# Written order on four more engines in the attention loop of a fused retention and mixture-of-experts kernel

## The chip, the cores and the metric

The kernel runs on one core of a Trainium2 chip. The metric is the device time of one execution in microseconds. Before the change three runs took 645.19, 640.9 and 643.24 us, median 643.24. A profile, taken of one more execution, lists every instruction of the five engines: TensorE (PE, with its weight loads as PEld), VectorE (DVE), ScalarE (ACT), GpSimd (POOL) and the load queue SyncE (SP), and the transfers of the DMA engines.

## The reference

Retention (a causal attention with a decay by distance in place of softmax) over 8 batches, 8 heads, 576 positions and 64 dimensions, then a mixture of experts over the 4608 resulting tokens of width 512, with 8 experts and one expert for each token:

```python
scores = scale * np.matmul(q, k.transpose(0, 1, 3, 2))
Dmat = np.where(rel >= 0, gamma[:, None, None] ** rel[None, :, :], 0.0)
x = np.matmul(scores * Dmat[None], v)          # then (B*S, H*D)
xn = x / (norm(x) + 1e-6); en = emb / (norm(emb) + 1e-6)
logits = xn @ en.T / tau
expert_idx = np.argmax(logits, axis=1)
gate_w = softmax(logits)[expert_idx]
out[mask_e] = gate_w * (relu(x[mask_e] @ w1[e]) @ w2[e])
```

All arithmetic is in float32.

## The kernel before, in words

**The attention loop** runs over the batches b = 0 to 7, and inside a batch over four pairs of heads. A pair of q and k, transposed, is one tile `qkt` of 576 KB (`load_qk`, L447); eight such tiles exist, so that batch b+1 loads into those of batch b-1. K and V in row form come as one transfer each (`load_k` L455, 1024 KB; `load_v` L460, 1152 KB), two buffers each.

For each pair, TensorE multiplies k and q in 128-wide chunks (`emit_A`, L590) into PSUM, and VectorE multiplies by the decay within a chunk (L599), which gives the masked scores in a `raw` tile. GpSimd scales q by its decay (`scale_q`, L579) in place, once A has read it. `emit_U` (L617; `emit_U0`, L639, in batch 0) forms k times v for each chunk, where k has been scaled by GpSimd (`scale_k`, L560, four steps; in batch 0 `turn_k`, L568 and L570, makes it from `qkt`). ScalarE copies the first chunk's result to `Tst` (L627, L647) and VectorE adds up the others (L629, L649). `emit_O` (L673) multiplies the masked scores by v, `emit_S` (L689) adds the state times scaled q, for two pairs at a time, and ScalarE copies x out (L699 to L702). The last 64 positions go apart: `emit_At` (L711, reads scaled q of all four pairs), its mask `pt` on VectorE (L713), `emit_Ot` (L728), copies L738.

**The router** works behind, in slots of the next two batches (`route_slots`): transposes of x tiles (`route_tile`, L754), a ScalarE copy to `y` (L758), a store to memory (L760, 256 KB each), sums of squares (L768), logits with the normalised expert matrix E (`route_logits`, L781, copies L784), a turn and sum (`route_turn`, L794, L797), the `head` (`route_head`, L174 to L182: seven small VectorE steps that find the best expert), then ranks (`route_rank`, L233 to L260), one-hots (`route_onehot`, L268 to L283), and a table (`route_table`, L296, L305, L307). E is made in batch 0 by `norm_E` (sum of squares, L534 to L538) and `build_E` (a GpSimd power L541, then VectorE L542 to L545). GpSimd's `build_g` (L520) makes the table `gsb` that `scale_q` uses.

In batches 3 to 6 one block of expert 0's first weight is loaded each (`w0_load`, L437), and split into two parts a batch later as written (`w0_split`: ScalarE cast L442, VectorE L443).

**The expert part** follows: for each expert, gathers, two chains of matmuls (L391, L951) and a scatter.

What sets the order: TensorE's instructions in the attention loop run in the order in which the code is written (`tc.manual_schedule` with TensorE alone). For the other engines and the load queue a planner picks among the instructions by its own estimate of what is ready; on the chip each engine then works through its list in order. All loads are issued from the SP queue, which is in order too: a transfer that must wait for a free buffer holds those behind it.

Of the kernel before, what the change touches and what calls it, by code (L numbers as in the profile page):

```python
# [18 lines left out]
P = 128  # L19
B, H, S, D = 8, 8, 576, 64  # L20
# [60 lines left out]
def retention_moe(ctx: ExitStack, tc: tile.TileContext, qk, kv, w1, w2, head, cst, out):  # L81
# [344 lines left out]
    with ExitStack() as att:  # L426
# [12 lines left out]
        def w0_split(c):  # L439
            hi, lo = (wslot[0][:, s, c * 1024 : (c + 1) * 1024] for s in range(2))  # L440
            raw = w0.pop(c)
            nc.scalar.copy(hi, raw)  # L442
            nc.vector.tensor_tensor(out=lo, in0=raw, in1=hi.bitcast(F32), op=ALU.subtract)  # L443

        def load_qk(b, p):
            t = qkp.tile([P, 2, S], F32, name="qkt")
            nc.sync.dma_start(out=t, in_=qk[b, p])  # L447
            qkt[b, p] = t

        kt, vt_ = {}, {}  # L450
# [13 lines left out]
        emb = cs[:, _FIRST : _FIRST + NP * NE].rearrange("p (r e) -> p r e", r=NP)  # L464
        taub = cs[:, _FIRST + NP * NE :]

        def load_decay(o, w):
            nc.sync.dma_start(out=cd[:, o : o + w], in_=cst[:, o : o + w])

        load_qk(0, 0)  # L470
        nc.sync.dma_start(out=cs, in_=head)
        load_decay(0, 2 * P)
        load_qk(0, 1)
        o = _C["g1"][0] - _FIRST
        load_decay(o, _CST.shape[1] - o)
        load_decay(2 * P, 2 * P)
        vt_[0] = a2.tile([P, KW + NP * D], F32, name="vt")
        v0 = vt_[0][:, :KW].rearrange("p (c n) -> p c n", c=NCH)
        v1 = kv[0, :, KW : 2 * KW].rearrange("p (c n) -> p c n", c=NCH)
        nc.sync.dma_start(out=v0[:, :, : DM // 2], in_=v1[:, :, : DM // 2])  # L480
        load_qk(0, 2)
        load_qk(0, 3)
        load_decay(4 * P, 4 * P + _C["decayt"][1])
        nc.sync.dma_start(out=v0[:, :, DM // 2 :], in_=v1[:, :, DM // 2 :])
        nc.sync.dma_start(out=vt_[0][:, KW:], in_=kv[0, :, 2 * KW :])
# [54 lines left out]
        def build_E():  # L540
            nc.gpsimd.tensor_tensor(out=en, in0=en, in1=half[:, :NE], op=ALU.pow)  # L541
            nc.vector.tensor_scalar(out=en, in0=en, scalar1=1e-6, scalar2=taub, op0=ALU.add, op1=ALU.mult)  # L542
            nc.vector.reciprocal(en, en)
            for p in range(NP):
                nc.vector.tensor_tensor(out=E32[:, p, :NE], in0=emb[:, p, :], in1=en, op=ALU.mult)  # L545
# [61 lines left out]
        def emit_U(b):  # L607
            k, v, T = kview(b), vview(b), Tst
            for c2 in range(NCH // 2):
                ps = psm.tile([P, 512], F32, name="m")  # L610
                u = ps.rearrange("p (c r d) -> p c r d", c=2, r=NP)
                for ci in range(2):
                    c = 2 * c2 + ci
                    for p in range(NP):
                        for h in range(2):
                            hd = 2 * p + h
                            nc.tensor.matmul(  # L617
                                u[h * D : (h + 1) * D, ci, p, :],
                                k[:, c, hd * D : (hd + 1) * D],
                                v[:, c, hd, :],  # L620
                                start=True,
                                stop=True,
                            )
                for ci in range(2):
                    c = 2 * c2 + ci
                    if c == 0:
                        nc.scalar.copy(T[:, 0], u[:, 0])  # L627
                    else:
                        nc.vector.tensor_tensor(out=T[:, c], in0=u[:, ci], in1=T[:, c - 1], op=ALU.add)  # L629
# [175 lines left out]
        def route_slots(b):  # L805

            G = group_tiles(b)[1]
            tiles = [lambda g=g: route_tile(b, g) for g in range(G)]
            rank, onehot = (lambda: route_rank(b)), (lambda: route_onehot(b))
            table, head = (lambda: route_table(b)), (lambda: route_head(b))  # L810
            logits, turn = (lambda: route_logits(b)), (lambda: route_turn(b))
            sq = route_squares
            if b == B - 2:
                gathers = [lambda i=i: gather(0, i, group_tiles(B - 1)[0] * P) for i in range(3)]
                return {
                    (b, 3): [logits] + tiles[:2] + [sq],
                    (b + 1, 0): [turn] + tiles[2:3] + [head, sq],
                    (b + 1, 1): [rank] + tiles[3:] + [sq],
                    (b + 1, 2): [onehot],
                    (b + 1, 4): [table, lambda: slots_to_tokens(0, 3)] + gathers + [route_bump],  # L820
                }
            return {
                (b + 1, 0): [logits] + tiles[:2] + [sq],
                (b + 1, 2): tiles[2:3] + [turn, head, sq],
                (b + 1, 3): tiles[3:] + [sq],
                (b + 2, 0): [rank, onehot],
                (b + 2, 2): [table],
            }

# [4 lines left out]
        def slot(b, k):  # L834
            for task in slots.pop((b, k), ()):
                task()

        ordered = tc.manual_schedule(engines={mybir.EngineType.PE})
        ordered.__enter__()
        for b in range(B):  # L840
            if b + 1 < B:
                load_qk(b + 1, 0)
                load_qk(b + 1, 1)
                load_v(b + 1)
                load_k(b + 1)
            if b == 0:
                build_g(0)
                build_g(1)
                emit_A(0, 0)
                turn_k(0)  # L850
                scale_q(0, 0)
                norm_E()
                emit_A(0, 1)
                turn_k(1)
                scale_q(0, 1)
                build_g(2)
                build_g(3)
                emit_O(0, 0)
                emit_U0(0)
                for p in (2, 3):  # L860
                    emit_A(0, p)
                    turn_k(p)
                    scale_q(0, p)
                build_E()
            else:
                for p in (0, 1):
                    emit_A(b, p)
                    scale_q(b, p)
                slot(b, 0)
                emit_U(b)  # L870
                emit_O(b, 0)
            if b >= 4:
                w0_split(b - 4)
            emit_S(b, 0)
            if b + 1 < B:
                load_qk(b + 1, 2)
                load_qk(b + 1, 3)
                scale_k(b + 1)
            if 3 <= b < 7:
                w0_load(b - 3)  # L880
            slot(b, 1)
            if b > 0:
                for p in (2, 3):
                    emit_A(b, p)
                    scale_q(b, p)
            slot(b, 2)
            emit_O(b, 1)
            if b == 0:
                emit_U0(1)
            slot(b, 4)  # L890
            emit_At(b)
            emit_S(b, 1)
            emit_Ot(b)
            slot(b, 3)
# [318 lines left out]
```

## Time and profile before

| What | Value |
|---|---|
| Runs, median (lowest to highest) | 643.24 us (640.9 to 645.19) |
| Profiled execution, its own time | 646.44 us |
| Its span | 644.6 us |
| PE, DVE, ACT, POOL busy | 608.1, 313.7, 237.7, 211.5 us |
| Mean granted TensorE clock | 0.964 |
| Moved by DMA | 110.08 MB, mean 171 GB/s |
| First score matmul of batches 1 to 6 | 34.65, 52.51, 71.03, 93.05, 117.16, 137.54 us |
| Logits of batch 6 (L781), behind its last attention matmul | 160.19 us |

A row of the order of time gives the start, the duration, the engine, the source line, the operation, output and inputs, and in brackets how long the engine had idled and what released it. A row of the stretches gives each engine's busy time in that stretch, the granted clock of TensorE as a share of full, the busy share of the 16 DMA engines and the rate. A row of waits gives who waited for whom, the total, the number of times and the longest. The profiled execution's own time is 3.2 us above the median of the runs.

### The profile page before, as it was taken

Reading aid. Unit: us, or ns where it says so; the run is one execution under the profiler, and the core shown is the slowest. Engines: PE = TensorE matmul, PEld = TensorE weight load, DVE = VectorE, ACT = ScalarE, POOL = GpSimd, SP = SyncE. Lnnn points to the kernel's source line nnn. Section 1 sums busy time; section 2 is a strip of 40 time slices with the busy share of each in tenths; the row PEclk is TensorE's granted clock in tenths of the full one; section 3 lists DMA queues with packets and bytes.
Section 4 is the critical chain, followed back from the end, with each engine's and each line's share of the span. In section 5 each row is a group of like instructions: output and inputs, shape, how many; then the busy total and the mean of one; then the engine's idle time right before and its main releaser. Section 6 shows DMA issues by size and latency. Waiting matters only on the chain. (4 is left out here: it accounts for less than half of the span.)

```text
span 644.6 us, 12800 instructions
## 1 busy us (share of the span) xinstructions
PE 608.1 (94%) x5250; PEld 545.1 (85%) x5250; DVE 313.7 (49%) x615; ACT 237.7 (37%) x466; POOL 211.5 (33%) x190
## 2 busy tenths in 40 slices
PE   6699978978979999999999999999999999999995
PEld 5587867867859889988998998899899889889985
DVE  6346646544736686570573367068236706812200
ACT  0034534543544445351543335144233424422211
POOL 4444442441215764413403231350323135020011
PEclk9889979887979999999999999999999999999999
DMA  8878878774225898483267149235615823700001
GB/s 312 315 270 313 299 282 313 262 293 167 100 97 170 259 189 296 130 224 137 81 136 269 40 115 271 94 99 131 245 39 122 263 98 110 149 36 26 1 34 43
DMA packets 73901, 110.08 MB, mean 171 GB/s; under 512 B 44362, under 2 KB 46062, under 8 KB 72048
## 3 DMA queue, kind: packets, MB, share of 16 engines
q1 hardware_dynamic: 66160, 89.28, 44.1%
q0 software_dynamic: 7680, 19.95, 9.5%
q8 instruction: 42, 0.69, 0.4%
q14 instruction: 19, 0.16, 0.1%
HBM read 80.62 MB, written 19.94 MB: 156 GB/s over the span
## 5 line engine op out<-in xcount | busy, mean ns | idle before, releaser
L391 PE MATMUL a<-xs,wslot 128*128 128x384 f32 (+1 forms) x1536 | 227.8, 309 | 0.0
L391 PEld LDWEIGHTS a<-xs,wslot 128*128 128x128 f32 x1536 | 225.9, 189 | 0.7
L951 PE MATMUL m<-wslot,hs 128*128 128x512 f32 (+1 forms) x984 | 222.0, 386 | 0.0
L951 PEld LDWEIGHTS m<-wslot,hs 128*128 128x128 f32 x984 | 181.1, 188 | 38.4
L925 DVE SCALAR_TENSOR_TENSOR hs<-a,hs 128x384 fp32r<-128x384 f32 (+1 forms) x128 | 62.8, 491 | 175.0 <-ACT hs L924 169.0
L959 POOL DMA_INDIRECT out<-y,sid x40 | 43.9, 1098 | 222.8 <-ACT y L958 186.7
L924 ACT ACTIVATE hs<-a 128x384 fp32r<-128x384 f32 (+1 forms) x128 | 56.2, 439 | 128.4 <-PE a L391 119.9
L149 DVE TENSOR_TENSOR wslot<-raw,wslot 128x1024 fp32r<-128x1024 f32 x60 | 73.3, 1222 | 27.2 <-ACT wslot L148 25.7
L148 ACT CAST wslot<-raw 128x1024 fp32r<-128x1024 f32 x60 | 62.7, 1045 | 38.0 <-DMA raw<-w 35.2
L958 ACT ACTIVATE y<-m,gt 128x512 f32<-128x512 f32 (+1 forms) x41 | 27.6, 676 | 109.9 <-PE m L951 88.8
L334 POOL DMA_INDIRECT raw<-xd,gid x40 | 41.6, 1039 | 75.0 <-DVE wslot L149 38.3
L599 DVE TENSOR_TENSOR raw<-a,cd 128x512 f32<-128x512 f32 x64 | 40.5, 685 | 41.0 <-PE a L590 40.9
L579 POOL TENSOR_TENSOR qkt<-qkt,gsb 128x448 f32<-128x448 f32 x32 | 36.0, 1139 | 63.1 <-PE a L590 44.5
L345 POOL DMA_INDIRECT gt<-gd,gid x40 | 50.4, 1260 | 12.2 <-issue 12.2
L673 PE MATMUL m<-raw,vt 128*64 128x128 f32 x512 | 35.6, 289 | 8.7 <-ACT y L758 4.2
L590 PE MATMUL a<-qkt 64*128 64x128 f32 x512 | 38.6, 305 | 2.7 <-DMA qkt<-qk 1.7
L560 POOL TENSOR_TENSOR kt<-kt,cs 128x512 f32<-128x512 f32 x28 | 28.4, 1043 | 36.1 <-DMA kt<-kv 25.2
L590 PEld LDWEIGHTS a<-qkt 64*128 64x128 f32 x512 | 34.9, 212 | 6.0 <-issue 2.3
L673 PEld LDWEIGHTS m<-raw,vt 128*64 128x64 f32 x512 | 30.4, 145 | 11.1 <-ACT y L758 4.6
L379 DVE COPY raw<-raw 128x1024 uint16<-128x1024 uint16 x37 | 28.1, 784 | 0.9 <-DMA raw<-raw 0.9
L372 DVE COPY raw<-raw 128x1024 uint16<-128x1024 uint16 x37 | 26.3, 725 | 0.0
L357 DVE TENSOR_TENSOR xs<-raw,xs 128x512 fp32r<-128x512 f32 x37 | 24.8, 685 | 0.3 <-ACT xs L356 0.3
(134 smaller groups left out, 396.2 us busy)
## 6 DMA issues: line engine op xcount, KB each, us to landing
raw<-w SPq DMA_DIRECT2D x64, 512.0 KB
qkt<-qk SPq DMA_DIRECT2D x32, 576.0 KB
xd<-y SPq DMA_DIRECT2D x36, 256.0 KB
vt<-kv SPq DMA_DIRECT2D x7, 1152.0 KB
kt<-kv SPq DMA_DIRECT2D x7, 1024.0 KB
vt<-kv SPq DMA_DIRECT2D x2, 512.0 KB
raw<-xd,gid POOLq DMA_INDIRECT x40
gt<-gd,gid POOLq DMA_INDIRECT x40
```

The source lines that it names most:

```text
L148: nc.scalar.copy(hi, raw)
L149: nc.vector.tensor_tensor(out=sl[:, 1, c * 1024 : (c + 1) * 1024], in0=raw, in1=hi.bitcast(F32), op=ALU.subtract)
L334: return nc.gpsimd.indirect_dma_start(out=t[:, :DM], out_offset=None, in_=xd[:rows, :], in_offset=bass.IndirectOffsetOnAxis(ap=gid[:, a : ...
L345: nc.gpsimd.indirect_dma_start(out=g[:, i : i + 1], out_offset=None, in_=gd[:, :], in_offset=bass.IndirectOffsetOnAxis(ap=gid[:, a : a + 1 ...
L391: nc.tensor.matmul(ps[:, :n], w[:, ws, d, f * P : (f + 1) * P], x[:, xsp, d, :], start=(d == 0 and k == 0), stop=(d == NP - 1 and k == 2),)
L590: nc.tensor.matmul(ps[h][:, c * P : (c + 1) * P], t[hs, 1, c * P : (c + 1) * P], t[hs, 0, c * P : (c + 1) * P], start=True, stop=True,)
L599: nc.vector.tensor_tensor(out=pm[:, h], in0=ps[h].rearrange("p (c n) -> p c n", c=NCH), in1=decay[:, 2 * p + h].unsqueeze(1).broadcast_to( ...
L673: nc.tensor.matmul(po[side(p, h), c * P : (c + 1) * P], v[:, c, 2 * p + h, :], pm[:, h, c, :], start=(c == 0), stop=False,)
L924: a = nc.scalar.activation(hi, ps[:, :n], AF.Relu)
L925: v = nc.vector.scalar_tensor_tensor(out=hs[:, 1, f, o : o + n], in0=ps[:, :n], scalar=0.0, in1=hi.bitcast(F32), op0=ALU.max, op1=ALU.subt ...
L951: nc.tensor.matmul(ps[:, :step], hs[:, hsp, f, i * P : (i + 1) * P], w[:, ws, f, n : n + step], start=(f == 0 and k == 0), stop=(f == NF - ...
L959: nc.gpsimd.indirect_dma_start(out=out[:, :], out_offset=bass.IndirectOffsetOnAxis(ap=sid[:, a : a + 1], axis=0), in_=y, in_offset=None, b ...
```

## The change

It puts ScalarE, VectorE, GpSimd and the load queue under the written order too, in the attention loop, and moves five pieces of the loop: `build_E` and `scale_k` go behind `emit_At`, one-hots of batches 0 to 5 go behind `emit_U` (a new slot 5), and `w0_split` goes between `emit_U` and `emit_O`. Ahead of the loop, the loads of pairs 1 to 3 of batch 0 and of the decay within a chunk (now one transfer of 256 KB in place of two) go on ScalarE's queue, the others stay on SP's. In the changed kernel the lines up to L464 keep their numbers, those of the attention loop are one lower and those of the expert part four higher.

```diff
-        def load_qk(b, p):
+        def load_qk(b, p, on=nc.sync):
             t = qkp.tile([P, 2, S], F32, name="qkt")
-            nc.sync.dma_start(out=t, in_=qk[b, p])
+            on.dma_start(out=t, in_=qk[b, p])
...
-        def load_decay(o, w):
-            nc.sync.dma_start(out=cd[:, o : o + w], in_=cst[:, o : o + w])
-
-        load_qk(0, 0)
-        nc.sync.dma_start(out=cs, in_=head)
-        load_decay(0, 2 * P)
-        load_qk(0, 1)
-        o = _C["g1"][0] - _FIRST
-        load_decay(o, _CST.shape[1] - o)
-        load_decay(2 * P, 2 * P)
+        def load_decay(o, w, on=nc.sync):
+            on.dma_start(out=cd[:, o : o + w], in_=cst[:, o : o + w])
+
...
+        o = _C["g1"][0] - _FIRST
+        load_qk(0, 0)
+        load_qk(0, 1, nc.scalar)
+        nc.sync.dma_start(out=cs, in_=head)
+        load_decay(0, 4 * P, nc.scalar)
+        load_decay(o, _CST.shape[1] - o)
+        load_qk(0, 2, nc.scalar)
         nc.sync.dma_start(out=v0[:, :, : DM // 2], in_=v1[:, :, : DM // 2])
-        load_qk(0, 2)
-        load_qk(0, 3)
+        load_qk(0, 3, nc.scalar)
...
-                (b + 2, 0): [rank, onehot],
+                (b + 2, 0): [rank],
+                (b + 2, 5): [onehot],
                 (b + 2, 2): [table],
...
-        ordered = tc.manual_schedule(engines={mybir.EngineType.PE})
+        E = mybir.EngineType
+        ordered = tc.manual_schedule(engines={E.PE, E.Activation, E.DVE, E.Pool, E.SP})
...
-                build_E()
             else:
...
                 emit_U(b)
+                slot(b, 5)
+                if b >= 4:
+                    w0_split(b - 4)
                 emit_O(b, 0)
-            if b >= 4:
-                w0_split(b - 4)
             emit_S(b, 0)
             if b + 1 < B:
                 load_qk(b + 1, 2)
                 load_qk(b + 1, 3)
-                scale_k(b + 1)
...
             emit_At(b)
+            if b == 0:
+                build_E()
+            if b + 1 < B:
+                scale_k(b + 1)
             emit_S(b, 1)
```

## The prediction

> **What bounds the kernel now.** I read the busy time stretch by stretch first, cut where the first score matmul (L590) of each batch of the attention loop starts; the last cut of the loop is where batch 6 hands over to the router (L781). Columns: length, busy time of each engine, granted TensorE clock, share of the DMA engines, GB/s.
>
> ```profile
> core 0 of [0], span 644.6 us
> core 0: us, PE busy (x) PEld busy (x) DVE busy (x) ACT busy (x) POOL busy (x), PEclk, DMA share, GB/s
> 0.00:34.65 34.65, 23.53 (x345) 20.61 (x345) 15.75 (x38) 3.64 (x7) 14.85 (x18) 0.85 0.79 292
> 34.65:52.51 17.86, 17.77 (x320) 15.29 (x316) 8.32 (x21) 7.56 (x24) 7.84 (x8) 0.90 0.85 304
> 52.51:71.03 18.52, 17.49 (x338) 15.15 (x337) 11.33 (x30) 9.03 (x24) 9.38 (x10) 1.00 0.88 310
> 71.03:93.05 22.02, 17.25 (x328) 14.85 (x327) 12.19 (x31) 10.29 (x28) 9.99 (x10) 0.92 0.82 295
> 93.05:117.16 24.11, 21.51 (x339) 19.10 (x338) 12.95 (x32) 9.89 (x23) 9.86 (x10) 0.79 0.74 261
> 117.16:137.54 20.38, 16.47 (x328) 14.17 (x327) 11.50 (x31) 10.24 (x28) 6.09 (x6) 0.99 0.85 310
> 137.54:160.19 22.65, 19.88 (x331) 17.63 (x330) 11.65 (x32) 8.79 (x20) 6.92 (x7) 0.80 0.64 228
> 192.00:644.60 452.60, 446.07 (x2532) 406.18 (x2530) 213.30 (x344) 162.11 (x274) 138.94 (x118) 1.00 0.47 136
> ```
>
> After 192 us TensorE works 446.07 of 452.60 us at full clock: the expert part has nothing to give and the change does not touch its order. The seven rows above it are another matter. At full clock an even batch is 17.49 us of TensorE (row 52.51) and an odd one 16.47 (row 117.16); the rest of each length is waiting, or work at half clock. Next, the order of time in batch 0, and around the longest stalls of batches 3 and 4.
>
> ```profile
> 4.59 1.16 PE L590 MATMUL a<-qkt 64*128 64x128 f32 x16 [0.30 <-DMA qkt<-qk]
> 8.49 1.16 PE L590 MATMUL a<-qkt 64*128 64x128 f32 x16 [1.36 <-DMA qkt<-qk]
> 10.07 0.20 DVE L543 RECIPROCAL en<-en 128x8 f32<-128x8 f32 x1
> 10.30 3.70 DVE L545 TENSOR_TENSOR E<-cs,en 128x8 f32<-128x8 f32 x4
> 14.66 2.35 PE L673 MATMUL m<-raw,vt 128*64 128x128 f32 x15 [2.88 <-DVE raw L599]
> 18.39 1.16 PE L590 MATMUL a<-qkt 64*128 64x128 f32 x16
> 25.64 0.45 PE L711 MATMUL a<-qkt 64*64 64x64 f32 x8
> 25.70 2.04 POOL L560 TENSOR_TENSOR kt<-kt,cs 128x512 f32<-128x512 f32 x2 [10.83 <-DMA qkt<-qk]
> 28.88 0.48 PE L711 MATMUL a<-qkt 64*64 64x64 f32 x4 [2.79 <-POOL qkt L579]
> 31.96 0.37 PE L711 MATMUL a<-qkt 64*64 64x64 f32 x2 [2.60 <-POOL qkt L579]
> ...
> 34.65 3.76 PE L590 MATMUL a<-qkt 64*128 64x128 f32 x32
> ```
>
> ```profile
> 78.05 0.49 SPq L437 DMA_DIRECT2D raw<-w  x1
> 78.63 0.52 SPq L455 DMA_DIRECT2D kt<-kv  x1
> ...
> 87.70 1.04 ACT L442 CAST wslot<-raw 128x1024 fp32r<-128x1024 f32 x1 [4.68 <-DMA raw<-w]
> 88.77 1.23 DVE L443 TENSOR_TENSOR wslot<-raw,wslot 128x1024 fp32r<-128x1024 f32 x1 [4.46 <-ACT wslot L442]
> 90.30 4.05 POOL L560 TENSOR_TENSOR kt<-kt,cs 128x512 f32<-128x512 f32 x4 [6.98 <-DMA kt<-kv]
> 90.48 0.41 DVE L713 TENSOR_TENSOR pt<-a,cd 128x256 f32<-128x256 f32 x1
> 90.95 0.49 PE L728 MATMUL m<-pt,vt 64*64 64x64 f32 x8 [4.77 <-DVE pt L713]
> 93.05 3.58 PE L590 MATMUL a<-qkt 64*128 64x128 f32 x32
> ...
> 110.50 1.98 PE L673 MATMUL m<-raw,vt 128*64 128x128 f32 x16 [2.00 <-ACT y L758]
> ```
>
> ```profile
> ACT wslot L442 <- DMA raw<-w: 17.2, 4, 4.7
> ```
>
> Three faults of order stand there. In batch 0 VectorE builds E (3.70 us) ahead of two decay masks, and L673 waits 2.88 us. GpSimd scales K of batch 1 ahead of q of pairs 2 and 3; that K came late, so L711 waits 2.79 and 2.60 us. In batches 3 to 6 ScalarE reaches the cast of an expert-0 weight block (L442) about 10 us after its load is issued, four times too soon (17.2 us); VectorE's L443 waits for ScalarE, and the mask `pt` or the copy of `y` that TensorE needs stands behind.
>
> **The change, part by part.** TensorE's own order is unchanged, so each gain is a wait that goes.
>
> *Batch 0.* E goes to the end of the batch on VectorE, GpSimd does all four q before any K. By hand, from the durations above: TensorE starts L590 of pair 0 at about 5.5 us, since a second queue now shares the engines; the sum of `sq`, now behind the first masks and K on VectorE, holds the norm matmul some 1.7 us; pair 1 starts near 9.7 and pair 2 near 15.0, where the row above says 18.39. From pair 2 to the first L711 took 7.25 us (25.64 less 18.39); that gives 22.3. Behind it, Tst, `pt` and the tail of L689 and L728 need some 2.7 us with nobody late. Batch 1 starts at 25.0 instead of 34.65: **9.6 us gained**. The loads cover this: at the rate of the next row 25 us hold about 8.8 MB, and batches 0 and 1 need 9.0 MB, the last of them pairs that batch 1 wants only 10 us later.
>
> ```profile
> 4.00:24.00 20.00, 15.02 (x202) 12.85 (x201) 14.01 (x28) 1.34 (x3) 7.45 (x7) 0.91 1.02 383
> ```
>
> *The two queues* alone I cost at nothing: the engines are full from 4 to 24 us (share 1.02), so a second queue brings pair 1 about 2 us sooner than 8.49 and pair 0 about 1 us later than 4.59, and `sq` eats the first.
>
> *The cast one batch later.* It now stands after the U matmuls of the batch after its load, more than 15 us after the transfer could land; its 1.04 us on ScalarE lie between Tst and the copies of x, where ScalarE idles (9 to 10 us busy of 20). So the four waits go, with the half-clock work behind them (L590 takes 3.58 us in batch 4, half of that at full clock). Six batches from 34.65 to 160.19 take 125.54 us; at full clock and without waits three odd and three even ones would be 16.4 + 17.5 + 16.4 + 17.5 + 16.4 + 16.4 = 100.6, the last without the 1.1 us of tile transposes behind the cut. **24.9 us can go.**
>
> *What comes in its place.* (a) E, built after `pt` while GpSimd scales K: the logits of batch 0 wait, and TensorE with them. Four E multiplies of 8 columns took 3.70 us beside GpSimd where a reciprocal took 0.20. With the steps ahead E is ready 4.4 us after `pt`, and TensorE has 2.9 us of scores and tail: 1.5 us. (b) L673 and its neighbours in even batches keep the 1.0 us of row 52.51 (18.52 less 17.49): 3 us. (c) The main term. These rows of batches 2 and 4 say how:
>
> ```profile
> 65.97 0.38 DVE L797 TENSOR_REDUCE L_all<-m 128x32 f32<-128x128 f32 x2
> 67.33 0.20 DVE L181 TENSOR_TENSOR oh<-wm,wme 128x40 bf16<-128x40 f32 x1
> 67.45 0.17 DVE L182 TENSOR_SCALAR tok_all<-wm 128x5 f32<-128x5 f32 x1
> 69.10 0.34 PE L728 MATMUL m<-pt,vt 64*64 64x64 f32 x8
> ```
>
> ```profile
> 111.50 4.04 POOL L560 TENSOR_TENSOR kt<-kt,cs 128x512 f32<-128x512 f32 x4 [4.44 <-DMA kt<-kv]
> 111.83 0.76 DVE L181 TENSOR_TENSOR oh<-wm,wme 128x40 bf16<-128x40 f32 x1
> 112.52 1.05 DVE L182 TENSOR_SCALAR tok_all<-wm 128x5 f32<-128x5 f32 x1
> ```
>
> Alone, L181 and L182 take 0.20 and 0.17 us; beside K scaling 0.76 and 1.05, each until one GpSimd step of 1.01 us ends. So far K of the next batch was scaled across the end of a batch (90.30 starts beside `pt`), behind the head. The changed kernel scales it right after the four q, which is when VectorE runs the route head, and `pt` now stands behind the whole head and the table sum. Four of the head's seven steps read two operands from SBUF or are of L182's kind. If all four wait, `pt` ends 4.9 us after the scaling starts, some 17.5 to 18 us into a batch, and L728 wants it at 16.6 (69.10 less 52.51), or 15.6 without the wait of (b): up to 2.5 us. If K lands after the head, nothing. The K transfer decides: it is the last of 3.7 MB (last stores, two pairs of q and k, V, K) that begin to flow about 2.8 us into the batch, and at 310 to 383 GB/s it lands 12.5 to 14.7 us in; the head starts at 13.5 (65.97 less 52.51) or a little sooner. I take 1.2 us in each of six batches: 7.2 us, bounds 0 and 15.
>
> The Trainium skill, SBUF — State Buffer, "SBUF: two separate sides", has the reason: VectorE and GpSimd share a port pair as an exclusive lock, which VectorE needs with two SBUF inputs. No row shows L175 or L177 beside GpSimd; by that rule they wait too, (c) would be near 12 us and the time near 631.
>
> (d) Half clock behind such stalls: 110.50 shows that a wait of 2.00 us (after a shorter one) brings it. Two of six batches at 1.7 us: 3.4, bounds 0 and 10. The Trainium skill, TensorE: Matmul & The Clock Gate, "Part 1: The HAM clock gate", puts the drop after an idle window of about 3.4 us; by it (d) would be 0 and the time 3.4 us lower, but here the measured 2.00 us decides. (e) In batch 7 VectorE now also splits a weight block (1.23 us) and does both rank and one-hot ahead of the last masks: 2 us later into the expert part.
>
> **Sum.** 9.6 + 24.9 − 1.5 − 3.0 − 7.2 − 3.4 − 2.0 = 17.4 us. Against the profiled execution (span 644.6, its own time 646.4) that is 629.0; the median of the runs, 643.2, lies 3.2 us lower, so **626 us**.
>
> Here is how the order moves where these terms rest. GpSimd at the start (gsb the decay table, qkt q, kt K, en the norm), before:
>
> ```order
> L541 TENSOR_TENSOR en<-en,half 128x8
> L520 TENSOR_TENSOR gsb<-cd 128x448 x2
> L579 TENSOR_TENSOR qkt<-qkt,gsb 128x448
> L520 TENSOR_TENSOR gsb<-cd 128x448
> L579 TENSOR_TENSOR qkt<-qkt,gsb 128x448
> L520 TENSOR_TENSOR gsb<-cd 128x448
> L560 TENSOR_TENSOR kt<-kt,cs 128x512 x2
> ```
>
> and now:
>
> ```order
> L519 TENSOR_TENSOR gsb<-cd 128x448 x2
> L578 TENSOR_TENSOR qkt<-qkt,gsb 128x448 x2
> L519 TENSOR_TENSOR gsb<-cd 128x448 x2
> L578 TENSOR_TENSOR qkt<-qkt,gsb 128x448 x2
> L540 TENSOR_TENSOR en<-en,half 128x8
> L559 TENSOR_TENSOR kt<-kt,cs 128x512 x4
> ```
>
> K and the norm go behind all q. VectorE in batch 4, from the masks (raw) into the head, before:
>
> ```order
> L599 TENSOR_TENSOR raw<-a,cd 128x512 x4
> L797 TENSOR_REDUCE L_all<-m 128x32
> L797 TENSOR_REDUCE L_all<-m 128x8
> L307 TENSOR_TENSOR tab<-m,tab 128x80
> L174 TENSOR_REDUCE mx<-L_all 128x5
> L443 TENSOR_TENSOR wslot_78<-raw,wslot_78 128x1024
> L175 TENSOR_TENSOR L_all<-L_all,mx 128x40
> ```
>
> and now, to `pt`:
>
> ```order
> L443 TENSOR_TENSOR wslot_78<-raw,wslot_78 128x1024
> L598 TENSOR_TENSOR raw<-a,cd 128x512 x4
> L796 TENSOR_REDUCE L_all<-m 128x32
> L796 TENSOR_REDUCE L_all<-m 128x8
> L174 TENSOR_REDUCE mx<-L_all 128x5
> L175 TENSOR_TENSOR L_all<-L_all,mx 128x40
> L177 SCALAR_TENSOR_TENSOR w<-L_all,wme 128x40
> L179 TENSOR_REDUCE wm<-w 128x5
> L181 TENSOR_TENSOR oh<-wm,wme 128x40
> L182 TENSOR_SCALAR tok_all<-wm 128x5
> L307 TENSOR_TENSOR tab<-m,tab 128x80
> L712 TENSOR_TENSOR pt<-a,cd 128x256
> ```
>
> The split has left the head and gone ahead of the masks; the table sum has gone behind the head.
>
> **Rivals.** *The head is not held*: K lands late enough, (c) and (d) vanish, the DMA engines are the next limit: their busy time in the six batches (share times length) is 15.2, 16.3, 18.1, 17.8, 17.3 and 14.5, together 99.2 us, no more than TensorE's 100.6. 626 − 10.6 gives 615 us; the 3.7 MB up to the end of K speak for it, the nearness in time against. *The loads pace it*: the in-order load queue now waits for the last stores of a batch ahead of the next q, 1 to 2 us idle per batch, and batches last 18.9 to 20 us; ten of the 24.9 us stay, 634 us. For it speaks the DMA share of 0.85 to 0.88 in good batches; against, that pairs 2 and 3 have 9 us to spare. *Slower than before*: K of batch b+1 is now issued only in batch b, where it was issued up to a batch ahead. U needs it scaled about 21 us after the batch that loads it began, 4.1 us of scaling included, so from a landing at 17 us each further us is one of TensorE. With 3.5 us and 1.7 us of half clock in all six batches 31 us are lost: 657 us. It needs a flight of 17 us from issue; the longest quoted, 78.63 to 90.30, is 11.7. *The casts still wait*, because their load is issued behind all others: only batch 0's part stays, 638 us; a whole batch of lead speaks against.
>
> **How the numbers follow.** Forecast 0.50, head not held 0.22, loads pace 0.18, casts still wait 0.04, slower 0.06. The bounds of (c) and (d) alone reach from 615 to 640; leaving out the tail of the last rivals, the range is 612 to 638. A measurement tells 1% (6.4 us) from no change: faster than 636.8 has 0.88 (of the first three cases' 0.90, 0.02 end above it), within 1% 0.06, slower 0.06.
>
> **What would show it.** Right: the first L590 of batch 1 near 25 us; no L442 waiting on its load; L728 waiting 0 to 2.5 us on `pt` in most batches, with L181, L175 or L182 near 1 us beside L559; batches of 17.5 to 20 us; the expert part still some 452 us. Wrong: batch 1 later than 28 us, U (L616) waiting for K, or L589 at a batch's start waiting for its q transfer.

## The result, and the profile after

The changed kernel takes **624.17 us** (median of four runs, 621.9 to 627.09) where the kernel before, run beside it, takes 642.07 (640.47 to 645.19): a ratio of 0.972, interval 0.965 to 0.978, so 17.9 us less. The profiled execution of the changed kernel has a time of 622.41 us and a span of 620.6. Against the profiled execution of before (646.44) that is 24.0 us less: before was caught 4 us above its median, after 2 us below. Terms below are on the scale of this pair.

The busy time by stretch, cut as in the prediction where the first score matmul of each batch starts (now L589; lines of the attention loop are one lower than before), and where batch 6 hands over to the router (L780):

```profile
core 0: us, PE busy (x) PEld busy (x) DVE busy (x) ACT busy (x) POOL busy (x), PEclk, DMA share, GB/s
0.00:26.56 26.56, 23.30 (x344) 20.51 (x344) 11.74 (x34) 3.68 (x7) 12.16 (x16) 0.94 0.89 341
26.56:44.26 17.70, 16.08 (x323) 13.70 (x316) 11.92 (x24) 7.95 (x24) 10.32 (x10) 1.00 0.84 307
44.26:64.06 19.80, 17.47 (x339) 15.08 (x338) 12.94 (x31) 8.96 (x22) 8.48 (x8) 1.00 0.78 287
64.06:80.53 16.47, 16.29 (x329) 14.17 (x328) 10.65 (x30) 9.11 (x27) 7.22 (x7) 1.00 0.93 342
80.53:98.87 18.34, 17.20 (x340) 14.90 (x339) 13.12 (x32) 10.06 (x25) 10.00 (x10) 1.00 1.00 377
98.87:115.85 16.98, 16.59 (x328) 14.36 (x327) 12.47 (x31) 10.31 (x28) 7.69 (x7) 1.00 0.96 345
115.85:132.36 16.51, 16.39 (x332) 14.22 (x331) 11.52 (x32) 8.71 (x20) 7.78 (x8) 1.00 1.01 374
132.36:168.00 35.64, 29.35 (x402) 23.66 (x403) 20.34 (x60) 17.61 (x46) 10.16 (x10) 0.86 0.31 104
168.00:620.60 452.60, 446.00 (x2531) 406.21 (x2529) 213.10 (x343) 162.28 (x274) 139.32 (x118) 1.00 0.47 136
```

Batch 1 starts 8.1 us sooner (26.56 for 34.65). The six batches last 105.80 us instead of 125.54, with full clock in every one: 19.7 us. What follows them takes 488.24 us instead of 484.41: 3.8 us given back, all of it ahead of the 452.60 us that are as they were. 8.1 + 19.7 − 3.8 = 24.0.

The cast is no longer waiting. Its group in the trace has no line of idle time ahead of it and nobody who waited for it; before, that stood at 17.2 us:

```profile
L442 ACT CAST wslot<-raw x4: 1046/1046/1049, 87.0 to 140.7; 128x1024 fp32r<-128x1024 f32 x4
its engine sat idle before it (us, times) until:
who waited for it (us, times):
```

The cost that the prediction put in its place is there too. Order of time at the end of batch 1, then of batch 3:

```profile
39.32 0.19 DVE L175 TENSOR_TENSOR L_all<-L_all,mx 128x32 f32<-128x32 f32 x1
39.51 4.04 POOL L559 TENSOR_TENSOR kt<-kt,cs 128x512 f32<-128x512 f32 x4 [0.81 <-DVE L_all L175]
39.54 1.06 DVE L177 SCALAR_TENSOR_TENSOR w<-L_all,wme 128x32 f32<-128x32 f32 x1
40.63 0.19 DVE L179 TENSOR_REDUCE wm<-w 128x4 f32<-128x32 f32 x1
40.86 0.75 DVE L181 TENSOR_TENSOR oh<-wm,wme 128x32 bf16<-128x32 f32 x1
41.53 1.05 DVE L182 TENSOR_SCALAR tok_all<-wm 128x4 f32<-128x4 f32 x1
43.05 0.34 PE L727 MATMUL m<-pt,vt 64*64 64x64 f32 x8 [1.62 <-DVE pt L712]
...
77.69 0.17 DVE L182 TENSOR_SCALAR tok_all<-wm 128x4 f32<-128x4 f32 x1
77.80 4.04 POOL L559 TENSOR_TENSOR kt<-kt,cs 128x512 f32<-128x512 f32 x4 [1.45 <-DMA kt<-kv]
79.06 0.34 PE L727 MATMUL m<-pt,vt 64*64 64x64 f32 x8
```

In batch 1 GpSimd begins to scale K in the middle of the route head; three head steps take 1.06, 0.75 and 1.05 us instead of 0.2, `pt` is late and TensorE waits 1.62 us. (The row puts GpSimd's 0.81 us of idle time there down to L175, so that it does not say when K landed; in batches 3 to 6 the K transfer is named.) In batch 3 K arrives 0.1 us after the last head step has begun: no step is held and nobody waits. The waits of L727 for `pt` are 1.62, 1.54, 0, 1.14, 0.39 and 0 us in batches 1 to 6, together 4.7.

### The profile page after: what moved, and what is told of

Its sections match the earlier page's. It is cut to its first block, busy times and chain, and to the rows that moved or that the text cites. A ratio compares the mean times of both kernels' runs of the same rounds, so it can differ in the third digit from the quotient of the medians.

```text
span 620.6 us, 12815 instructions
## 1 busy us (share of the span) xinstructions
PE 598.7 (96%) x5250; PEld 536.8 (86%) x5250; DVE 317.8 (51%) x615; ACT 238.7 (38%) x466; POOL 213.1 (34%) x190
## 5 line engine op out<-in xcount | busy, mean ns | idle before, releaser
L598 DVE TENSOR_TENSOR raw<-a,cd 128x512 f32<-128x512 f32 x64 | 39.9, 683 | 24.2 <-PE a L589 24.2
L672 PE MATMUL m<-raw,vt 128*64 128x128 f32 x512 | 34.6, 289 | 2.7 <-DVE raw L598 2.7
L589 PE MATMUL a<-qkt 64*128 64x128 f32 x512 | 35.3, 285 | 1.8 <-DMA qkt<-qk 1.0
L589 PEld LDWEIGHTS a<-qkt 64*128 64x128 f32 x512 | 31.4, 192 | 4.9 <-issue 2.9
L672 PEld LDWEIGHTS m<-raw,vt 128*64 128x64 f32 x512 | 30.6, 146 | 4.5 <-issue 3.5
L357 DVE TENSOR_TENSOR xs<-raw,xs 128x512 fp32r<-128x512 f32 x37 | 24.8, 686 | 0.9 <-ACT xs L356 0.9
```

Of the source, the lines that this page charges most:

```text
L589: nc.tensor.matmul(ps[h][:, c * P : (c + 1) * P], t[hs, 1, c * P : (c + 1) * P], t[hs, 0, c * P : (c + 1) * P], start=True, stop=True,)
L598: nc.vector.tensor_tensor(out=pm[:, h], in0=ps[h].rearrange("p (c n) -> p c n", c=NCH), in1=decay[:, 2 * p + h].unsqueeze(1).broadcast_to( ...
L672: nc.tensor.matmul(po[side(p, h), c * P : (c + 1) * P], v[:, c, 2 * p + h, :], pm[:, h, c, :], start=(c == 0), stop=False,)
```

## The experiments

Each time is a median. In brackets stands its ratio to the kernel before, run beside it on the same chip, with a 95% interval. Kernels that ran on different chips are compared by what they gain on the kernel before beside them. The changed kernel gains 17.9 us in the result and 20.6 us when run again, so differences of two or three microseconds between chips decide nothing.

**The changed kernel again.**

> The changed kernel once more, as the measure for the other kernels of this call. Every theory: 622 to 627 us, and in its profile batch 1 starts at 26 to 27 us. The theory that a race between the K transfer and the route head decides each stall on `pt` expects the stalls to move between batches from execution to execution, since the transfer's landing moves by more than a microsecond; their sum should stay between 3 and 7 us. A rival, that the order of VectorE alone makes them, expects them in the same batches (1, 2, 4 and a little in 5) with the same lengths (1.62, 1.54, 1.14, 0.39 us).

623.21 us (0.9685, interval 0.964 to 0.973), 20.6 us below the kernel before (643.83). In its profile batch 1 starts at 28.85 us, 2 us later than expected, so batch 0 differs by as much from one execution to the next. L727 waits 2.35 us in batch 1, 1.67 in batch 2 and nothing in batches 3 to 6, together 4.0. That the waits of batches 4 and 5 are gone is what a race with the K transfer would give. Batch 2 is no race: in both profiles GpSimd starts on K right behind q, with no idle time (57.80 and 60.46 us), so K had landed, and the wait is there both times.

**First loads back on one queue.**

```
-        load_qk(0, 1, nc.scalar)
-        load_decay(0, 4 * P, nc.scalar)
-        load_qk(0, 2, nc.scalar)
-        load_qk(0, 3, nc.scalar)
+        (the first loads of the kernel before, all on nc.sync, in their old order)
```

> The changed kernel with the first loads back on SP's queue, in the old order; all else unchanged. Theory of the prediction: the two queues are worth nothing, because the DMA engines are full from 4 to 24 us anyway: the time stays within 2 us of the changed kernel, batch 1 starts between 25.5 and 28 us. Rival: the second queue makes most of the 8.1 us that batch 0 gained; then batch 1 starts at 30 us or later and the time is 4 to 8 us longer. Third possibility: the second queue costs something, since the first transfer lands at 5.3 us instead of 4.6 us; then this kernel is 1 to 2 us faster.

619.21 us (0.961, 0.957 to 0.966): 4.0 us **faster** than the changed kernel beside it (six runs each, 615.82 to 623.60 against 621.09 to 627.59). It is the third possibility, at twice its size. The edit also brings back the old order of the transfers and the decay in two parts, so it tests the three together. The start of both, the changed kernel first; with the old loads the attention loop has the line numbers of the kernel before again:

```profile
5.34 2.08 PE L589 MATMUL a<-qkt 64*128 64x128 f32 x16 [1.02 <-DMA qkt<-qk]
6.84 0.28 DVE L503 TENSOR_SCALAR ident<-cs 128x128 f32<-128x128 f32 x1 [5.51 <-DMA cs<-head]
9.75 1.06 PE L536 MATMUL m<-sq,onef 128*128 128x8 f32 x8 [1.29 <-DVE sq L533]
10.74 1.16 PE L589 MATMUL a<-qkt 64*128 64x128 f32 x16
12.67 3.34 PE L672 MATMUL m<-raw,vt 128*64 128x128 f32 x32
```

```profile
4.55 1.16 PE L590 MATMUL a<-qkt 64*128 64x128 f32 x16 [0.23 <-DMA qkt<-qk]
4.75 0.29 DVE L504 TENSOR_SCALAR ident<-cs 128x128 f32<-128x128 f32 x1 [3.42 <-DMA cs<-head]
7.80 1.06 PE L537 MATMUL m<-sq,onef 128*128 128x8 f32 x8 [1.51 <-DVE sq L534]
8.79 1.16 PE L590 MATMUL a<-qkt 64*128 64x128 f32 x16
10.47 1.97 PE L673 MATMUL m<-raw,vt 128*64 128x128 f32 x32
```

SP issues pair 0 and then `cs` as its first two transfers in both. With ScalarE's queue beside it pair 0 lands 0.8 us later and `cs` 2.1 us later; from `cs` hang the identity, the transposes of K, `sq` and the norm matmul, and pair 1's scores stand behind that on TensorE. They begin 1.95 us later (10.74 for 8.79); another 1.4 us is the next L672, which takes 3.34 us for 1.97, near half clock. Batch 1 starts at 22.99 us here, and at 24.16 and 25.57 in the two later kernels with one queue (in the first of them the norm has moved too); with two it starts at 26.56, 28.85, 28.33, 26.93 and 28.72 in the five whose batch 0 is that of the change. The means, 24.2 and 27.9, differ by 3.6 us.

A part of that is lost again behind batch 0. The six batches last longer here than in the changed kernel (105.80 and 105.17 us):

```profile
22.99:131.15 108.16, 102.64 (x1981) 88.37 (x1975) 71.69 (x177) 55.36 (x142) 54.94 (x52) 0.98 0.91 342
```

Batch 1 now comes before its K: U (L617) waits 0.31 and 0.32 us for the scaling, and the clock of batches 1 and 2 falls to 0.98 and 0.93.

**Constants first on SP's queue, still two queues.**

```
+        nc.sync.dma_start(out=cs, in_=head)
         load_qk(0, 0)
         load_qk(0, 1, nc.scalar)
-        nc.sync.dma_start(out=cs, in_=head)
```

> The changed kernel with its two queues, but the block of constants `cs` is issued ahead of pair 0 on SP's queue. With one queue batch 1 started at 22.99 us, with two at 26.56 and 28.85. Theory one: with two queues the identity's constants land 2.1 us later (L503 at 6.84 instead of 4.75 us), and that chain (identity, transposes of K, `sq`, norm) makes all of the loss: then `cs` first gives back 3 to 4 us, and batch 1 starts near 23.5 us. Theory two: the engines are shared between the queues, so what is wanted first comes later whatever the order; pair 0 now lands 0.5 us later and 0.5 to 1 us is gained, half clock in batch 0 stays: within 1.5 us of the changed kernel, batch 1 at 25.5 to 28 us.

624.38 us (0.970, 0.965 to 0.975), as the changed kernel. `cs` now lands by 3.88 us, and pair 0 not before 7.20, where TensorE waits for it:

```profile
7.20 2.08 PE L589 MATMUL a<-qkt 64*128 64x128 f32 x16 [2.88 <-DMA qkt<-qk]
```

The time is that of theory two; batch 1 at 30.46 us is even later than it said. In both orders what comes second on SP's queue lands late: `cs` at 6.84 us for 4.75, pair 0 at 7.20 for 4.55. The Trainium skill, DMA: Bandwidth & Descriptors, "Issuing engines are not separate DMA queues", says that transfers started by several engines share the same 16 DMA engines and interleave, and that starting them on several engines saves only issue time. These runs agree that the engines are shared, and add a price: 3.6 us in batch 0. The rate did rise a little: between 4 and 24 us it is 406 and 407 GB/s in the two profiles of the changed kernel and 390 with one queue. More bytes came, and those that were wanted first came later.

**The cast in the same batch as its load again.**

```
-                if b >= 4:
-                    w0_split(b - 4)
...
             slot(b, 2)
+            if 3 <= b < 7:
+                w0_split(b - 3)
```

> The changed kernel, but the cast and split of an expert-0 weight block stand in the same batch as its load again (after the second slot of batches 3 to 6), as the scheduler had put them before. Theory of the prediction: ScalarE waits again for the load, 3 to 5 us in each of four batches, VectorE's split and the mask `pt` behind it, TensorE 2 to 5 us each with half clock behind: 10 to 20 us slower than the changed kernel, so 634 to 644 us, in batches 3 to 6 alone. Rival: what helped the loop is the written order of the loads (they now arrive sooner), and the cast finds its block landed: then within 3 us of the changed kernel.

650.60 us (1.011, 1.007 to 1.014): 27.4 us slower than the changed kernel, more than expected, and 6.8 us slower than before. The end of batch 3:

```profile
85.53 1.04 ACT L442 CAST wslot<-raw 128x1024 fp32r<-128x1024 f32 x1 [7.03 <-DMA raw<-w]
86.61 1.22 DVE L443 TENSOR_TENSOR wslot<-raw,wslot 128x1024 fp32r<-128x1024 f32 x1 [6.90 <-ACT wslot L442]
88.22 0.49 PE L727 MATMUL m<-pt,vt 64*64 64x64 f32 x8 [7.31 <-DVE pt L712]
90.33 3.04 PE L589 MATMUL a<-qkt 64*128 64x128 f32 x32
```

It is the whole chain of the prediction: load, cast, split, `pt`, TensorE, half clock (L589 3.04 us for 2.06). The cast waits 23.8 us in four times, and the six batches last 133.79 us with a granted clock of 0.91. Batches 3 to 6 alone are long (23.1 to 24.6 us). Without this move nothing is left of the loop's gain: before, the six batches lasted 125.54 us. The cast stands at one place of the batch here, behind its second slot; at another the price could differ.

**K of batch 1 ahead of q of pairs 2 and 3, in batch 0 alone.**

```
                 build_g(3)
+                scale_k(1)
...
-            if b + 1 < B:
+            if 0 < b < B - 1:
                 scale_k(b + 1)
```

> The changed kernel, but in batch 0 GpSimd scales K of batch 1 ahead of q of pairs 2 and 3, as before the change; later batches unchanged. Theory of the prediction: GpSimd waits for that K, which lands near 17 to 20 us or later, then works 4.1 us on it, and At (L710) of pairs 2 and 3 waits 2 to 3 us each: batch 1 starts 4 to 7 us later and the time is 4 to 8 us longer. Rival: K lands early with the new load order and GpSimd's order in batch 0 does not matter: within 2 us.

Three of four runs took 625.79 to 628.89 us, median 627.23, which is 4.0 us slower than the changed kernel and at the lower end of the theory; the fourth took 636.0, and the median of all four is 628.06. Batch 1 starts at 32.99 us.

```profile
24.18 4.04 POOL L559 TENSOR_TENSOR kt<-kt,cs 128x512 f32<-128x512 f32 x4 [8.31 <-DMA kt<-kv]
29.36 0.48 PE L710 MATMUL a<-qkt 64*64 64x64 f32 x4 [4.34 <-POOL qkt L578]
```

GpSimd stands 8.31 us before a K that lands at 24 us (17 to 20 were expected), with q ready behind it; TensorE pays 4.34 us and another 0.61.

**The written order, with nothing moved.**

```
-        ordered = tc.manual_schedule(engines={mybir.EngineType.PE})
+        E = mybir.EngineType
+        ordered = tc.manual_schedule(engines={E.PE, E.Activation, E.DVE, E.Pool, E.SP})
```

> The kernel before with only the wider manual schedule: all five engines follow the program text, which is that of before; nothing is moved, first loads on SP. Theory: the written order by itself gains nothing, the moves do. In that text K of the next batch is scaled ahead of q of pairs 2 and 3, and GpSimd now has to keep to it: K lands 12 to 15 us into a batch, the four steps of 1.01 us end near 17 to 19 us, and At (L711) wants those q near 15 us: 3 to 5 us of wait and 1 to 2 us of half clock in each of six batches, against that the four waits of 4 to 5 us for the casts gone: 645 to 670 us, not faster than before. Rival: keeping to the program text is what brought the gain, and the moves are trimmings: 620 to 630 us.

654.52 us (1.016, 1.010 to 1.021): 9.8 us slower than before, as the theory said. The end of batch 1:

```profile
39.51 4.04 POOL L560 TENSOR_TENSOR kt<-kt,cs 128x512 f32<-128x512 f32 x4 [8.48 <-DVE mx L174]
44.69 0.48 PE L711 MATMUL a<-qkt 64*64 64x64 f32 x4 [4.06 <-POOL qkt L579]
```

Holding the engines to the program text makes the text's order count, and this text has K ahead of q: L711 waits 3.2 to 4.3 us in every batch from 1 to 6, and the six batches last 140.21 us at a clock of 0.86. The casts, which the text has a batch later, wait no more. The planner had it the other way round: K behind q, which is good, and the cast too soon. The loop needs both orders; with either missing it is longer than before (133.79 and 140.21 us for 125.54). Not tried are the moves with TensorE alone held to the text. GpSimd's idle time of 8.48 us is put down to VectorE here; in the other six scalings, 49.0 us in all, to the K transfer. K starts to be scaled 12.8 us into the batch (39.51 less 26.69).

**The route head behind `pt`.**

```
-                (b + 1, 2): tiles[2:3] + [turn, head, sq],
+                (b + 1, 2): tiles[2:3] + [turn, sq],
+                (b + 1, 6): [head],
...
             emit_At(b)
+            slot(b, 6)
```

> The changed kernel, with the route head of batches 1 to 6 moved on VectorE from before the mask `pt` to behind it (behind At in the program). Theory: TensorE's waits for `pt` (4.7 us in one profile) go, since `pt` no longer stands behind head steps that GpSimd's K scaling holds up; 3 to 5 us faster than the changed kernel, 618 to 621 us; the head steps of 1 us stay, where nothing waits for them. Rival one: the wait then moves to the next use of VectorE, the masks of the next batch (L598), or to the copies of Tst; time within 1.5 us. Rival two: the head's result is wanted by the rank of the next batch, and it is the tail of the loop that pays: slower.

619.88 us (0.961, 0.958 to 0.965), as the theory said: 3.3 us below the changed kernel run again, and 4.2 us when each is taken against the kernel before beside it (24.8 and 20.6 us less). Batch 1 of this kernel, and a wait in batch 2:

```profile
40.32 4.04 POOL L559 TENSOR_TENSOR kt<-kt,cs 128x512 f32<-128x512 f32 x4 [0.65 <-DMA kt<-kv]
41.78 0.42 DVE L712 TENSOR_TENSOR pt<-a,cd 128x256 f32<-128x256 f32 x1 [1.76 <-PE a L710]
42.33 1.08 DVE L175 TENSOR_TENSOR L_all<-L_all,mx 128x32 f32<-128x32 f32 x1
42.35 0.34 PE L727 MATMUL m<-pt,vt 64*64 64x64 f32 x8
...
61.72 0.27 PE L727 MATMUL m<-pt,vt 64*64 64x64 f32 x1 [0.68 <-issue]
```

The head steps are still held (L175 1.08 us), but `pt` now waits for its scores alone and TensorE does not wait for `pt`. The six batches last 103.42 us, 1.8 and 2.4 us less than in the two profiles of the changed kernel, where 4.0 and 4.7 us of waits for `pt` have gone. So rival one holds in part. In batch 2 L727 waits 0.68 us and the profile names no releaser (`issue`); the wait ends where ScalarE's two copies of x end (L698, 1.07 us from 60.64). The same wait stands in both later kernels with this edit. That the copies hold it is not shown.

**No scaling of K for batches 2 to 7.**

```
-            if b + 1 < B:
-                scale_k(b + 1)
+            if b == 0:
+                scale_k(1)
```

> The changed kernel without the scaling of K for batches 2 to 7 on GpSimd (this part of the computation is left out); the route head stays ahead of `pt`. It takes away what is said to hold the head's steps. Theory of the prediction: L177, L181 and L182 take 0.2 us each in all batches, `pt` is in time and L727 waits 0 us for it in batches 1 to 6: 3 to 5 us faster than the changed kernel, much as with the head behind `pt`. Rival: the stalls on `pt` come from the place of the head alone, or from At that ends late; then L727 still waits 1 to 1.6 us in batches 1, 2 and 4 and the time is within 1.5 us.

619.01 us (0.959, 0.955 to 0.964), 4.2 us below the changed kernel run again, or 5.1 us by the kernels before. L727 waits for `pt` in none of batches 1 to 6, with the head still ahead of it. So the stall needs both: the head in front and GpSimd's K scaling beside it. The six batches are the shortest of all and the clock is full:

```profile
28.72:130.18 101.46, 100.19 (x1982) 86.54 (x1976) 64.89 (x181) 54.63 (x142) 27.99 (x25) 1.00 0.96 351
```

**E behind its norm again.**

```
                 norm_E()
+                build_E()
                 emit_A(0, 1)
...
-            if b == 0:
-                build_E()
```

> The changed kernel with E built right behind its norm in batch 0 again, ahead of the masks of pair 1 on VectorE and of q of pair 1 on GpSimd. Theory of the prediction: GpSimd's power (1.67 us) and VectorE's E (0.4 us alone, up to 3.7 us beside GpSimd) push the masks of pair 1 back by 2 to 5 us, L672 waits 1 to 3 us: batch 1 starts 2 to 4 us later, time 2 to 4 us longer. Rival: in the changed kernel these masks have slack, or the loads set batch 0: within 1.5 us.

624.53 us (0.970, 0.965 to 0.975; six runs from 619.99 to 629.03), not told apart from the changed kernel: 1.3 us above it by the medians and 2.4 us by the kernels before, with runs nine microseconds apart. Its profile shows the wait that the theory names, 2.01 us of L672 for a mask at 17.46, and batch 1 at 31.18; but that execution is at the upper end of the runs (628.75). What E's move is worth stays open.

**Two repairs together.** One queue, and the head behind `pt`; the edits are shown above.

> The changed kernel with two edits alone: first loads on one queue, and the route head behind `pt`. Theory: the two gains add up, 7.3 to 8 us below the changed kernel, 615 to 616.5 us; batch 1 starts near 23 us and no L728 waits for `pt` in batches 1 to 6. Rival: what the head loses in batches 1 and 2 is lost there again to K and q that come late, 618 to 620 us.

616.51 us (0.958, 0.955 to 0.961), at the upper edge of the theory: of 7.3 us expected, 6.7 came by the medians (623.21 less 616.51), and 5.6 by the kernels before. Batch 1 starts at 25.57 us, not near 23. No L728 waits for `pt` in batches 1 to 6, and the six batches last 102.67 us, so what one queue lost in batches 1 and 2 does not return here.

**Four repairs.** Added are, in batch 7, the rank behind the last masks and the last split behind At, and in batch 0 the norm behind the first outputs.

```
-                    (b + 1, 1): [rank] + tiles[3:] + [sq],
-                    (b + 1, 2): [onehot],
+                    (b + 1, 1): tiles[3:] + [sq],
+                    (b + 1, 2): [rank, onehot],
...
-                norm_E()
                 emit_A(0, 1)
...
                 emit_O(0, 0)
+                norm_E()
...
-                if b >= 4:
+                if 4 <= b < 7:
                     w0_split(b - 4)
...
             slot(b, 6)
+            if b == 7:
+                w0_split(3)
```

> The changed kernel with the first loads on one queue, the route head behind `pt` in batches 1 to 6, in batch 7 the rank behind the last masks and the last weight split behind At, and in batch 0 the norm matmul (`sq`) behind the first outputs instead of between the scores of pairs 0 and 1. Theory: the four costs are separate and add up: 4.0 us for the queue and 3.3 to 4.2 us for the head (measured), 2 to 4 us in batch 7 (L673 waited 2.7 us for its mask, half clock behind), 1 to 1.5 us for `sq`: 610 to 614 us. Rival: the loads are the limit once batch 1 starts at 22 us; it waits for K and q, the loop does not get shorter than with one of the two edits, 616 to 620 us.

**613.69 us** (0.956, 0.952 to 0.960), in the theory's range: 29 us below the kernel before beside it (642.72), 9.5 below the changed kernel run again, or 8.4 by the kernels before. Batch 7 of the changed kernel, and then of this one:

```profile
144.86 1.22 DVE L443 TENSOR_TENSOR wslot<-raw,wslot 128x1024 fp32r<-128x1024 f32 x1
146.30 0.79 DVE L244 TENSOR_TENSOR run<-run,s 128x8 bf16<-128x8 bf16 x1
148.35 2.48 DVE L598 TENSOR_TENSOR raw<-a,cd 128x512 f32<-128x512 f32 x4
149.19 3.60 PE L672 MATMUL m<-raw,vt 128*64 128x128 f32 x32 [2.70 <-DVE raw L598]
```

```profile
139.42 2.48 DVE L599 TENSOR_TENSOR raw<-a,cd 128x512 f32<-128x512 f32 x4 [0.28 <-PE a L590]
140.62 2.42 PE L673 MATMUL m<-raw,vt 128*64 128x128 f32 x32
144.69 0.32 PE L296 MATMUL m<-rp,bt 128*128 128x80 bf16 x4 [1.65 <-DVE rp L283]
```

The wait of 2.70 us for the last masks is gone, and the half clock behind it (3.60 us for 2.42). A wait of 1.65 us for the one-hot takes its place further on. From the hand-over of batch 6 to the end it is 484.14 us, where the changed kernel has 488.24, the kernel with two repairs 487.46 and before 484.41. Rank and split moved together; the kernel with the cast in its load's batch has no split in batch 7 and still waits 2.05 us there, so the larger part is the rank's. The norm's place brought nothing that shows: batch 1 starts at 24.16 us, and the 1.5 us that `sq` had held became a wait of 2.10 for pair 1's transfer.

## Why the prediction came out as it did

**The time.** 624.2 stood against 626 forecast, but the terms were further off than that. On the profiled pair 17.4 us were forecast and 24.0 came. The runs show 17.9 us, because the two profiled executions lay at opposite sides of their medians; that the medians agree so closely is partly luck. The costs (a) to (d) in the loop were forecast at 15.1 us and came to 5.2; batches 0 and 7 took 3.3 of the difference back.

**Two readings.** ScalarE does not reach the first cast about 10 us after its load is issued: it starts it 9.65 us after (87.70 less 78.05), and had stood idle for 4.68 of these. And L590 takes 2.06 us at full clock, not half of 3.58. Neither enters the sum.

**Batch 0: 9.6 forecast, 8.1 measured in one profile and 5.8 in the other.** The hand-worked start of batch 1 was 25.0, the profiles say 26.56 and 28.85. GpSimd's order was rightly named (4.0 us when undone). The step that failed is *"the two queues alone I cost at nothing"*. The reason that I gave, that the engines are full from 4 to 24 us, was the reason for a loss: a full set of engines shared by a second queue brings what is wanted first later. I saw pair 0 come a microsecond later and did not follow `cs`, 2.1 us later, down its chain. It cost 3.6 us in batch 0 and 4.0 us of the time; the near agreement is partly chance, since the one-queue kernel loses some again in batches 1 and 2.

**The waits and the half clock of batches 1 to 6: 24.9 could go, and they went.** The six batches last 105.80 us against 100.6 without any wait; the rest, 5.2 us, is in the main the 4.7 on `pt` and one wait of 0.79 us in batch 2. Putting the cast back costs 27.4 us. The prediction names the cast alone here; the written order also needs K's scaling behind q in these batches, as the kernel with nothing moved shows.

**(a) E, 1.5 forecast:** nothing in two profiles, in one of them by a hair. E's multiplies took 1.81 us in one execution and 0.40 in the other; in the first they end at 28.49 us and the logits (L780) begin at 28.55. With the head behind `pt` they took 1.92 us, and the logits 1.55 us for 1.10. The 3.70 us of before was taken beside GpSimd's table and q steps, and I carried it to a place where less ran beside it.

**(b) The 1.0 us in even batches, 3.0 forecast:** it stood in batch 2 alone (0.79 us, and 0.34 in the second profile). The prediction put the 1.0 us of row 52.51 at L673 and its neighbours; but in the kernel before, too, it stood at L590 (1.01 us at 63.56, no releaser named). What makes it stays open; it was not tried.

**(c) `pt` behind a held head, 7.2 forecast, bounds 0 and 15:** 4.7 and 4.0 us of waits in two profiles; 3.3 to 4.2 us of time by the head moved, 4.2 to 5.1 by the scaling left out. The mechanism is shown from both sides; its size was put too high. The race was rightly placed: K was expected 12.5 to 14.7 us into the batch, and its scaling begins between 12.95 (39.51 less 26.56) and 14.61 us in (130.46 less 115.85). The head (L174) begins 12.5 to 14.0 us in, where I took 13.5 or a little sooner, and its steps take 1.2 us when none is held; in batches 3 and 6 it begins at 12.62 and 13.54 and is all but over when K lands. The Trainium skill's rule on the port pair (SBUF — State Buffer, "SBUF: two separate sides") was right about the steps for which I had no row: L175 takes 1.08 us and L177 1.06 beside GpSimd, 0.19 alone; the reduction L179 between them stays at 0.19. The 631 us that I drew from it were wrong, since the scaling mostly begins in the middle of the head or after it: it held 3, 4, 0, 2, 1 and 0 steps in batches 1 to 6 of one profile and 4, 4, 0, 0, 0 and 0 of the other.

**(d) Half clock behind such stalls, 3.4 forecast:** none; all six batches show a clock of 1.00. The rule that I took from before, that a wait of 2.00 us brings it, does not hold by length alone (below).

**(e) Batch 7, 2.0 forecast:** 3.8 in this pair, and 2.1 to 3.9 in the nine profiles with this order (486.49 to 488.27 us from the hand-over to the end, 484.41 before). The mechanism was right, split and rank ahead of the last masks; I left out the half clock behind the wait. Undoing it brings the stretch to 484.14 us.

**The rivals.** *The head is not held* (615) is the kernel without K scaling, and that takes 619.0, with the two queues and batch 7 as they are. *The loads pace it* did not come: no score matmul of batches 1 to 6 waits for its q, at a DMA share of 1.00 and 1.01 in batches 4 and 6. The batches of 18.9 to 20 us that I named for it would not have told it from the forecast, which itself adds up to 115.7 us for the six, 19.3 each. *Slower*: in the changed kernel U never waits for K.

## What to carry to other kernels

Where an engine works in the order written, each step belongs behind everything that is ready sooner, and a step that waits for a transfer may belong one stage later than looks natural. Here the cast in its load's batch cost 27 us, and with K's scaling ahead of q the written order was slower than the planner's. Where the DMA engines are already full, a second load queue brought a few per cent more rate here and a later start; look at what is wanted first, and follow it down its chain before costing the edit at nothing. Where VectorE and GpSimd work side by side, put what TensorE waits for ahead of the VectorE steps that GpSimd holds, as long as nobody waits for those.

## What the runs showed of the hardware

The length of one wait does not tell whether TensorE's clock drops. Behind a wait of 2.35 us (the changed kernel again, batch 1) the next 32 score matmuls took 2.06 us, full clock; behind one of 1.78 us (one queue, batch 1) they took 3.37. In both, TensorE had been at full clock up to the wait:

```profile
46.03 0.34 PE L727 MATMUL m<-pt,vt 64*64 64x64 f32 x8 [2.35 <-DVE pt L712]
47.24 2.06 PE L589 MATMUL a<-qkt 64*128 64x128 f32 x32
```

```profile
41.17 0.34 PE L728 MATMUL m<-pt,vt 64*64 64x64 f32 x8 [1.78 <-DVE pt L713]
42.67 3.37 PE L590 MATMUL a<-qkt 64*128 64x128 f32 x32
```

So here a term for half clock could only be carried as a chance. The idle window of about 3.4 us that the Trainium skill gives (TensorE: Matmul & The Clock Gate, "Part 1: The HAM clock gate") is longer than either wait, and longer than the 2.70 us in batch 7 behind which L672 ran at half clock.

The same kernel's batch 0 ends at 26.56 us in one execution and 28.85 in another, and the first score matmuls take 2.08 us in the one and 1.16 in the other. A single profile of the start does not carry a term of two microseconds.
